# Attention and a maxout FFN in one kernel: batch 0 and its loads rearranged, and two pairs a turn from batch 2 on

## The chip, the cores and the metric

The kernel runs on one core of a Trainium2 chip. Five engines work in parallel, each with a queue of its own that it goes through in order: TensorE (PE: matmuls and transposes, results into PSUM), VectorE (DVE), ScalarE (ACT: exp, log), GpSimd (POOL) and SyncE (SP: issues DMAs). They wait for each other through semaphores. The metric is the device time of one execution in microseconds (us). Less is better.

## The reference

The inputs are q, k, v of 8 batches, 12 heads, 448 tokens and 64 dims. Attention has one more term in the denominator of the softmax, and its output is the input of an FFN with three up-projections, of which the largest counts:

```python
scores = q @ k.T / sqrt(64);  m = max(scores)
e = exp(scores - m)
attn = e / (sum(e) + exp(-m) + 1e-09)
x = (attn @ v), heads side by side        # 3584 x 768
h = maximum(maximum(x @ w1, x @ w2), x @ w3)
out = h @ w_out                           # all weights 768 x 768
```

Since exp(-m) is one more exponential of zero, the kernel works without the maximum: e / (sum(e) + 1) with e = exp(scores).

## The kernel before

**Pairs.** Work goes by pairs of heads: 6 pairs a batch, 48 in all, one to a turn of the main loop (`it`). The 448 keys of a head are 3 chunks of 128 and a last one of 64. Scores are made transposed (keys on the partitions). For a chunk of 128 keys two matmuls of 64 rows each run side by side on the two halves of the array, one per head: these are the half-array matmuls (64x448 in the profile; `scores`, L239). The last chunks of both heads go together as one matmul over the full array (`scores_last`, L255). `exp_scores` (L249) is one ScalarE exp of 896 columns per chunk, into `eT`; `exp_last` (L265) one of 448, into `eL`.

**Sums.** `av_main` (L273) multiplies with v and a block of ones beside it, so that one head's output and its denominator come out of the same six full matmuls. `av_last` (L285) adds the last chunk with two half-array matmuls. `reciprocals` takes 1/(sum+1) as exp(-ln(sum+1)) on ScalarE (L298, L299); `normalize` (L307, VectorE) writes the batch's `xT`. Batch 0 has a form of its own (`sums_main`, `sums_last`, `reciprocals_one`, `normalize_one`).

**FFN.** When a batch's six pairs are done, `batch_done` puts its groups on a list: 18 `up_group`s (six full matmuls each, L356, closed by VectorE with a copy, L370, or a maximum, L372) and 6 or 8 `out_group`s (six matmuls, L390, then VectorE, L415, and a DMA out). `group()` takes the next one off the list; the turns of the next batch call it 3 to 5 times, between the steps of attention, so that TensorE has work while ScalarE and VectorE finish. Batch 0 has no groups to fill in, and uses `keep_busy` (L349), matmuls on zeros.

**Queues.** The order on each engine is the order in which the program is written out (`manual_schedule`). q, k, v of a pair come by DMA from SP's queue (`load`, L92 and L93: two DMAs for each of q, k, v) into three raw buffers of three pairs each. Weights come from POOL's queue (`load_weight`, L147); they are converted to fp16 on the way. In the profile q1 is the DMA queue of SP and ScalarE, q0 that of POOL. VectorE casts q and k to fp16 (`cast_qk`: L183, L184, L189) and POOL scales v (`scale_v`, L157). Up to pair 11 TensorE transposes q and k (`transposes`, L221, L226; VectorE copies them out into `qkT`, L233); from pair 12 on a DMA does (L209).

**PSUM.** Three pools of two buffers: `s` (scores, also the last chunk's), `av` (sums), `u` (groups and transposes). A buffer comes free when its reader is done. A turn in the steady part of before is

```python
scores(p,0..1); group(); av_main(prev); av_last(prev)
scores(p,2); scores_last(p); reciprocals(prev); exps
group(); normalize; group(); normalize; further groups
```

The order in batch 0 (L470 to L508), the first turn of batch 1 (L509 to L530) and the initial loads (L97 to L114) is written out by hand.

Of the kernel before, what the change touches and what calls it, by code (L numbers as in the profile page):

```python
# [21 lines left out]
def kernel(  # L22
# [44 lines left out]
    out_pool = ctx.enter_context(tc.tile_pool(name="outp", bufs=3))  # L67
# [8 lines left out]
    NRAW = 3  # L76
    HB = NPAIR // 2
# [24 lines left out]
    load(1, 2, "v")  # L102
    load(3, 1, "qk")
    load(4, 2, "q")
    load(3, 1, "v")
    load(4, 2, "k")
# [6 lines left out]
    nc.vector.memset(raw[2][0][64:128, 0:2, NB, :], 0.0)  # L113
# [24 lines left out]
    eT = cpool.tile([128, 2, NB, 2, S], MMDT, name="eT")  # L138
# [22 lines left out]
    def casts(p):  # L161
        cast_qk(p)
        scale_v(p)

    def cast_qk(p):
        qt, kt, _ = raw[(p // HB) % NRAW]
        h0 = 2 * (p % HB)
        hs = slice(h0, h0 + 2)
        k6, q6 = k16[p % NK], q16[p % NK]
        if p == 0:  # L170

            nc.scalar.copy(out=k6[:, 0:NB], in_=kt[:, hs, 0:NB].rearrange("p h c d -> p c h d"))
            for eng, cs in ((nc.scalar.copy, slice(0, 2)), (nc.vector.tensor_copy, slice(2, NB + 1))):
                eng(out=q6[:, cs], in_=qt[:, hs, cs].rearrange("p h c d -> p c h d"))
        else:
            if p >= P_DMA and (p // NPAIR) % 2:

                nc.vector.tensor_copy(
                    out=q6[:, 1 : NB + 1], in_=qt[:, hs, 0:NB].rearrange("p h c d -> p c h d")
                )  # L180
                nc.vector.tensor_copy(out=q6[64:128, 0], in_=qt[0:64, hs, NB])
            else:
                nc.vector.tensor_copy(out=q6, in_=qt[:, hs].rearrange("p h c d -> p c h d"))  # L183
            nc.vector.tensor_copy(  # L184
                out=k6[:, 0:NB], in_=kt[:, hs, 0:NB].rearrange("p h c d -> p c h d")
            )
        for hh, half in enumerate(halves):
            last = nc.gpsimd if p == 0 else nc.vector
            last.tensor_copy(out=k6[half, NB, hh], in_=kt[0:64, h0 + hh, NB])  # L189
# [14 lines left out]
    def transposes(p):  # L204
        odd = (p // NPAIR) % 2
        qkT = att_pool.tile([2 * D, 1024], MMDT, tag="qkT", bufs=3)
        qkTs[p] = qkT, 0, S
        if p >= P_DMA:
            nc.sync.dma_start_transpose(  # L209
                out=qkT.rearrange("q (c p) -> q c p", p=128),  # L210
                in_=qk16[p % NK].rearrange("p c h d -> p (c h d)"),
            )
            qkTs[p] = qkT, 64 * odd, 512
            return
        trT = ps_u.tile([128, 1024], MMDT, tag="u", name="trT")


        order = (NB, 0, 1, 2) if odd else (0, 1, 2, NB)
        n0 = 0
        for c in order:  # L220
            nc.tensor.transpose(  # L221
                out=trT[:, n0 : n0 + 128], in_=q16[p % NK][:, c], identity=ident16
            )
            n0 += SL if c == NB else 128
        for c in range(NB + 1):
            nc.tensor.transpose(  # L226
                out=trT[:, S + c * 128 : S + c * 128 + 128], in_=k16[p % NK][:, c], identity=ident16
            )
        if p == 0:
            nc.vector.tensor_copy(out=qkT[:, 0 : S + 128], in_=trT[:, 0 : S + 128])  # L230
            nc.scalar.copy(out=qkT[:, S + 128 : S + 512], in_=trT[:, S + 128 : S + 512])
        else:
            nc.vector.tensor_copy(out=qkT[:, 0 : S + 512], in_=trT[:, 0 : S + 512])  # L233
# [14 lines left out]
    def exp_scores(p, c, stp):  # L248
        nc.scalar.activation(out=eT[:, p % 2, c], in_=stp[:, :, 0:S], func=AF.Exp, scale=scale)  # L249
# [13 lines left out]

    def exp_last(p, stl):
        nc.scalar.activation(out=eL[:, p % 2], in_=stl[:, 0, 0:S], func=AF.Exp, scale=scale)  # L265
# [3 lines left out]
    def av_main(p, hh, av=None):  # L269
        if av is None:  # L270
            av = ps_av.tile([128, 512], FP32, tag="av", name="av")
        for c in range(NB):
            nc.tensor.matmul(  # L273
                out=av[:, 0:S],
                lhsT=vst[:, p % VB, hh * NB + c, (1 - hh) * D : (3 - hh) * D],
                rhs=eT[:, p % 2, c, hh, :],
                start=(c == 0),
                stop=False,
            )
        return av  # L280
# [32 lines left out]
    def sums_main(p, ps, ones):  # L313
        for c in range(NB):
            for hh, half in enumerate(halves):
                nc.tensor.matmul(  # L316
                    out=ps[half, 0:S],
                    lhsT=vst[:, p % VB, hh * NB + c, (1 - ones) * D : (2 - ones) * D],
                    rhs=eT[:, p % 2, c, hh, :],
                    start=(c == 0),  # L320
                    stop=False,
                )
# [10 lines left out]
    def reciprocals_one(den):  # L333
        lnd = small.tile([128, S], FP32, tag="lnd")
        rb = small.tile([128, S], FP32, tag="rb")
        nc.scalar.activation(out=lnd, in_=den[:, 0:S], func=AF.Ln, bias=1.0)
        nc.scalar.activation(out=rb, in_=lnd, func=AF.Exp, scale=-1.0)
        return rb
# [108 lines left out]
    LEFT = 4  # L447
    keep_busy(13)
    casts(0)
    transposes(0)  # L450
    keep_busy(3)
    for it in range(NP + 1):
        p = it if it < NP else None
# [5 lines left out]
        first = {3: 1, 4: 2}.get(it)  # L459
        if first is not None:  # L460
            hs = slice(2 * first, 2 * first + 2)
            nc.vector.memset(raw[2][0][64:128, hs, NB - 1 : NB + 1, :], 0.0)
            if first == 1:
                load(NPAIR, 1, "v")
            load(NPAIR + first, 1)
        if it in (3, 4):
            load_weight(0, it - 3)
        if it in (5, 6, 8):
            load_weight((5, 6, 8).index(it) + 1)
        if it < NPAIR:  # L470

            casts(it + 1)
            for c in range(2):
                exp_scores(p, c, scores(p, c))
            if prev is None:
                keep_busy(3)
                exp_scores(p, 2, scores(p, 2))
                transposes(1)
                exp_last(p, scores_last(p))
            else:  # L480
                den, av = (ps_av.tile([128, 512], FP32, tag="av", name=n) for n in ("den", "av"))
                sums_main(prev, den, 1)
                stp = scores(p, 2)
                sums_main(prev, av, 0)
                stl = scores_last(p)
                sums_last(prev, den, 1)
                sums_last(prev, av, 0)
                exp_scores(p, 2, stp)
                exp_last(p, stl)
                rb = reciprocals_one(den)  # L490
                transposes(it + 1)
            if it < NPAIR - 1:
                keep_busy(3)
            else:

                ups = [up_open()]
                up_part(ups[0], 0, 0, 0, range(3))
                av5 = ps_s.tile([128, 2, 512], FP32, tag="s", name="av5")
                sums_main(p, av5[:, 1], 1)
                sums_main(p, av5[:, 0], 0)  # L500
                sums_last(p, av5[:, 1], 1)
                sums_last(p, av5[:, 0], 0)
                rb5 = reciprocals_one(av5[:, 1])
            if prev is not None:
                normalize_one(prev, av, rb)
            if it == NPAIR - 1:
                normalize_one(p, av5[:, 0], rb5)
                batch_done(0)  # L508
        elif it == NPAIR:  # L509
            exp_scores(p, 0, scores(p, 0))  # L510

            up_part(ups[0], 0, 0, 0, (3,))
            ups.append(up_open())
            up_part(ups[1], 0, 0, 1, range(4))
            ups.append(up_open(ps_av, "av"))
            up_part(ups[2], 0, 0, 2, range(4))
            for dc in (4, 5):
                for fc, ps in enumerate(ups):
                    up_part(ps, 0, 0, fc, (dc,))
                    if dc == 5:  # L520
                        up_close(ps, 0, 0, fc)
            del queue[0:3]
            exp_scores(p, 1, scores(p, 1))
            group()
            casts(it + 1)
# [5 lines left out]
        else:  # L531
            late = it + 1 < P_DMA
            if not late:

                if it + 2 < NP:
                    cast_qk(it + 2)
                    transposes(it + 2)
                if it + 1 < NP:
                    scale_v(it + 1)
            if p is not None:  # L540
                for c in range(2):
                    exp_scores(p, c, scores(p, c))
            group()
            if late:
                casts(it + 1)
            avs = [av_main(prev, hh) for hh in range(2)]
            av_last(prev, avs)
            if p is not None:
                stp = scores(p, 2)
                stl = scores_last(p)  # L550
            rb = reciprocals(prev, avs)
            if p is not None:
                exp_scores(p, 2, stp)
                exp_last(p, stl)
# [6 lines left out]
            if it % NPAIR == 0:  # L561
                batch_done(prev // NPAIR)
# [3 lines left out]
            for _ in range(n_groups - 3):  # L566
                group()

        for n in range(NPAIR + HB, 2 * NPAIR) if it == NPAIR else (it + 5,):
            if it >= NPAIR and n < NP:  # L570
                load(n, 1)
# [32 lines left out]
```

## Time and profile before

| | |
|---|---|
| median of 3 runs | 367.63 us (367.45 to 368.14) |
| the profiled execution | 367.07 us, span 365.3 us |
| TensorE busy | 357.4 us (98%) |
| VectorE busy | 243.4 us (67%) |
| ScalarE busy | 221.1 us (61%) |
| GpSimd busy | 53.6 us (15%) |
| up matmuls (L356) | 864, 175.3 us |
| out matmuls (L390) | 336, 59.3 us |
| sums with v (L273) | 252, 54.5 us |
| scores (L239) | 288, 44.1 us |
| keep-busy (L349) | 34, 10.1 us |
| DMA | 58.61 MB, mean 160 GB/s |

The span runs from the first to the last instruction. The shown duration of a matmul holds the time that it takes to pass through the array, and matmuls overlap: the time that one costs is read from the start of one to the start of the next. "Idle before" tells how long an engine stood still ahead of a group of instructions, and who released it.

### The profile page before, as it was taken

The numbers are of one execution on the slowest core, as the hardware profiler recorded it, in microseconds if no ns is written. First come the engines' busy times: TensorE is split into PE (matmuls) and PEld (weight loads), VectorE is DVE, ScalarE is ACT, GpSimd is POOL, SyncE is SP. The second block draws the span as 40 slices with busy tenths as digits, with TensorE's granted clock in tenths as the row PEclk, the third lists the DMA queues.
The fourth block names the chain that finished last, engine by engine and source line by source line (L and its number), as shares of the span: only waits on it lengthen the run. The fifth ranks groups of instructions, "written<-read, shape, count | busy, mean of one in ns | idle before, by whom it ended". The sixth has DMA issues, their size and how long they took to land.

```text
span 365.3 us, 6122 instructions
## 1 busy us (share of the span) xinstructions
PE 357.4 (98%) x2086; PEld 163.9 (45%) x2086; DVE 243.4 (67%) x521; ACT 221.1 (61%) x335; POOL 53.6 (15%) x159
## 2 busy tenths in 40 slices
PE   8999999999999999999999999999999999999995
PEld 3434444444444444444444444444444444445552
DVE  4474777876578677577657867757666776555553
ACT  4996476765666766666567666666566766651000
POOL 4263112211211211211121121121112112000000
PEclk9999999999999999999999999999999999999999
DMA  5999997668667888849764896758675673005006
GB/s 151 229 234 229 233 247 211 155 177 214 161 180 182 208 184 154 195 107 185 182 173 122 178 200 164 175 133 214 159 174 137 165 208 83 5 2 131 2 0 172
DMA packets 87951, 58.61 MB, mean 160 GB/s; under 512 B 43504, under 2 KB 84464, under 8 KB 87920
## 3 DMA queue, kind: packets, MB, share of 16 engines
q1 hardware_dynamic: 83632, 53.18, 59.7%
q0 software_dynamic: 3920, 4.72, 7.5%
q10 hardware_dynamic: 368, 0.33, 0.4%
q8 instruction: 16, 0.26, 0.3%
q14 instruction: 15, 0.12, 0.1%
HBM read 42.47 MB, written 11.01 MB: 146 GB/s over the span
## 4 chain that ended last, share of the span: by engine, by line
PE 91%; ACT 2%; DMA 2%; DVE 2%; issue 1%; SPq 0%; DVEq 0%
PE up L356 44%; PE op L390 15%; PE av L273 13%; PE stp L239 8%; PE stl L255 4%; PE av L285 3%; DMA kin<-in_k_dram 2%; PE busy L349 2%; ACT eT L249 1%; PE trT L221 1%; PE trT L226 1%; PE av L316 1%; DVE qkT L233 1%; DVE o_sb L415 0%; DVE qk L183 0%
## 5 line engine op out<-in xcount | busy, mean ns | idle before, releaser
L356 PE MATMUL up<-xT,w 128*128 128x448 f16 x864 | 175.3, 353 | 0.7 <-DVE xT L307 0.4
L249 ACT ACTIVATE eT<-stp 128x896 f16<-128x896 f32 x144 | 125.5, 910 | 53.3 <-PE stp L239 53.3
L356 PEld LDWEIGHTS <-w 128*128 128x128 f16 x864 | 81.7, 98 | 81.7 <-issue 12.5
L372 DVE TENSOR_TENSOR hT<-hT,up 128x448 f16<-128x448 f16 x96 | 59.6, 621 | 52.1 <-PE up L356 51.1
L157 POOL TENSOR_SCALAR vst<-vin 128x384 f16<-128x384 f32 x132 | 43.1, 338 | 255.2 <-issue 159.2
L298 ACT ACTIVATE lnd<-av 64x448 f32<-64x448 f32 x84 | 45.3, 539 | 49.0 <-PE av L285 48.0
L390 PE MATMUL op<-w,hT 128*128 128x384 f16 x336 | 59.3, 326 | 0.0
L273 PE MATMUL av<-eT,vst 128*128 128x448 f16 x252 | 54.5, 352 | 0.0
L307 DVE TENSOR_TENSOR xT<-av,rb 64x448 f16<-64x448 f32 x84 | 51.8, 617 | 1.4
L239 PE MATMUL stp<-qkT 64*128 64x448 f16 x288 | 44.1, 353 | 1.5 <-DVE qkT L233 0.7
L370 DVE CAST hT<-up 128x448 f16<-128x448 f32 x48 | 29.8, 624 | 22.9 <-PE up L356 22.2
L415 DVE TENSOR_SCALAR o_sb<-op 128x384 f32<-128x384 f32 (+1 forms) x56 | 30.8, 550 | 20.0 <-PE op L390 19.0
L390 PEld LDWEIGHTS <-hT 128*128 128x128 f16 x336 | 31.6, 98 | 24.7 <-issue 4.0
L273 PEld LDWEIGHTS <-vst 128*128 128x128 f16 x252 | 24.7, 98 | 22.4
L184 DVE CAST qk<-kin 128x384 f16<-128x384 f32 x47 | 25.7, 548 | 1.1 <-DMA kin<-in_k_dram 0.7
L265 ACT ACTIVATE eL<-stl 128x448 f16<-128x448 f32 x48 | 25.9, 539 | 0.0
L299 ACT ACTIVATE rb<-lnd 128x448 f32<-128x448 f32 x42 | 24.2, 576 | 1.3
L239 PEld LDWEIGHTS <-qkT 64*128 64x128 f16 x288 | 11.0, 94 | 23.2 <-issue 16.5
L419 ACT ACTIVATE o_sb<-op 128x192 f32<-128x192 f32 x1 | 0.3, 331 | 30.2 <-DVE o_sb L415 30.2
L189 DVE CAST qk<-kin 64x64 f16<-64x64 f32 x94 | 17.5, 187 | 1.3
L255 PE MATMUL stl<-qkT 128*128 128x448 f16 x48 | 17.4, 362 | 0.0
L285 PE MATMUL av<-eL,vst 64*128 64x448 f16 x84 | 15.2, 359 | 0.0
(50 smaller groups left out, 117.7 us busy)
## 6 DMA issues: line engine op xcount, KB each, us to landing
out_dram<-o_sb SPq DMA_DIRECT2D x54, 192.0 KB, 2.8
qin<-in_q_dram SPq DMA_DIRECT2D x46, 128.0 KB, 3.0
kin<-in_k_dram SPq DMA_DIRECT2D x45, 128.0 KB, 2.9
vin<-in_v_dram SPq DMA_DIRECT2D x44, 128.0 KB, 2.9
kin<-in_k_dram SPq DMA_DIRECT2D x46, 96.0 KB, 2.7
qin<-in_q_dram SPq DMA_DIRECT2D x45, 96.0 KB, 2.7
vin<-in_v_dram SPq DMA_DIRECT2D x44, 96.0 KB, 2.8
w<-in_moe_w_dram POOLq DMA_DIRECT2D x2, 1152.0 KB, 17.1
```

Source lines behind the costliest of these rows:

```text
L157: nc.gpsimd.tensor_scalar(out=out, in0=in_, scalar1=LAMBDA, scalar2=1.0, op0=ALU.mult, op1=ALU.mult)
L239: nc.tensor.matmul(out=stp[:, hh, 0:S], lhsT=qkT[hh * D : hh * D + D, k0 + c * 128 : k0 + c * 128 + 128], rhs=qkT[hh * D : hh * D + D, q0 ...
L249: nc.scalar.activation(out=eT[:, p % 2, c], in_=stp[:, :, 0:S], func=AF.Exp, scale=scale)
L255: nc.tensor.matmul(out=stl[:, 0, 0:S], lhsT=qkT[:, k0 + NB * 128 : k0 + NB * 128 + 128], rhs=qkT[:, q0 : q0 + S], start=True, stop=True,)
L273: nc.tensor.matmul(out=av[:, 0:S], lhsT=vst[:, p % VB, hh * NB + c, (1 - hh) * D : (3 - hh) * D], rhs=eT[:, p % 2, c, hh, :], start=(c == ...
L298: nc.scalar.activation(out=lnd[mine], in_=avs[hh][other, 0:S], func=AF.Ln, bias=1.0)
L307: nc.vector.tensor_tensor(out=xTs[b][mine, j, :], in0=avs[hh][mine, 0:S], in1=rb[mine], op=ALU.mult)
L356: nc.tensor.matmul(out=ps[:, 0:S], lhsT=w_sb[i][:, dc, ts(fc, 128)], rhs=xTs[b][:, dc, :], start=(dc == 0), stop=(dc == NDC - 1),)
L370: nc.vector.tensor_copy(out=h, in_=ps[:, 0:S])
L372: nc.vector.tensor_tensor(out=h, in0=h, in1=ps[:, 0:S], op=ALU.max)
L390: nc.tensor.matmul(out=ps[:, 0:NW], lhsT=hTs[sb][:, fc, ts(t, 128)], rhs=wout_sb[:, fc, ts(nh, NW)], start=(fc == 0), stop=(fc == NFC - 1),)
L415: nc.vector.tensor_scalar(out=o_sb[:, cs], in0=src, scalar1=1.0 / LAMBDA, scalar2=None, op0=ALU.mult)
```

## The change

**Loads and buffers.** The raw buffers become four of two pairs each (`NRAW`, `HB`), the output tiles five instead of three, `eT` three instead of two. The initial loads take v of pairs 1 and 2, and k of pairs 4 and 5, one by one (four DMAs more on SP), and k of 4 and 5 stands before v of 3. Pair 7's q and k, then v of 6 and 7, then pair 8's q and k are issued in turns 4, 5 and 6, each behind a small VectorE memset of a part of the tile that the load then writes. v of 8 and 9 and q, k of 9 follow in turn 7; from turn 8 on every load is of two pairs.

**Weights.** The first half of w1 is issued on POOL in turn 3 behind `scale_v(3)` and a VectorE memset of one of its columns, the second half at the start of turn 4, w2, w3 and w_out at the start of turns 5, 6 and 8. `scale_v(p)` moves from turn p-1 into turn p, up to pair 11.

**Batch 0.** In turn p the next pair's transposes and its first scores are written out before the sums of the previous pair with v; the normalise moves into the next turn; `keep_busy` stays in turn 0 alone. Pair 5's sums, the first three up groups of batch 0 and pair 6's transposes (in a buffer of the `s` pool) follow each other in turn 5. Pair 4's transposes are copied out in two parts.

**From pair 12 on** a turn takes two pairs. The half-array matmuls stand in three stretches: `av_last(p-1)` with scores 0 and 1 of p; score 2 of p with score 0 of p+1; `av_last(p)` with scores 1 and 2 of p+1. The last chunks of both pairs share one PSUM buffer and one exp (`scores_last2`, `exp_last2`). A turn calls `group()` 8 to 10 times.

The diff, cut:

```diff
-    NRAW = 3
-    HB = NPAIR // 2
+    NRAW = 4
+    HB = 2
...
     load(2, 1, "qk")
-    load(1, 2, "v")
+    load(1, 1, "v")
     load(3, 1, "qk")
+    load(2, 1, "v")
     load(4, 2, "q")
+    load(4, 1, "k")
+    load(5, 1, "k")
     load(3, 1, "v")
-    load(4, 2, "k")
     load(4, 2, "v")
...
+    def scores_last2(p):
+        stl = ps_s.tile([128, 2, 512], FP32, tag="s", name="stl")
+        for n in range(2):
+            qkT, q0, k0 = qkTs[p + n]
+            nc.tensor.matmul(
+                out=stl[:, n, 0:S],
+                lhsT=qkT[:, k0 + NB * 128 : k0 + NB * 128 + 128],
+                rhs=qkT[:, q0 : q0 + S],
...
+    def exp_last2(stl):
+        nc.scalar.activation(out=eL, in_=stl[:, :, 0:S], func=AF.Exp, scale=scale)
...
-        first = {3: 1, 4: 2}.get(it)
-        if first is not None:
-            hs = slice(2 * first, 2 * first + 2)
-            nc.vector.memset(raw[2][0][64:128, hs, NB - 1 : NB + 1, :], 0.0)
-            if first == 1:
-                load(NPAIR, 1, "v")
-            load(NPAIR + first, 1)
-        if it in (3, 4):
-            load_weight(0, it - 3)
+        if it in (4, 5, 6):
+            t = (raw[NRAW - 1][0], raw[NRAW - 1][2], raw[0][0])[it - 4]
+            hs = slice(0, 2) if it == 6 else slice(2, 4)
+            nc.vector.memset(t[64:128, hs, NB - 1 : NB + 1, :], 0.0)
+            p_new, n_new, names = ((NPAIR + 1, 1, "qk"), (NPAIR, 2, "v"), (NPAIR + 2, 1, "qk"))[it - 4]
+            load(p_new, n_new, names)
+        if it == 4:
+            load_weight(0, 1)
         if it in (5, 6, 8):
             load_weight((5, 6, 8).index(it) + 1)
...
+                last = it == NPAIR - 1
+                late = it == 3
+                if last:
+                    normalize_one(*waiting)
+                else:
+                    cast_qk(it + 1)
+                scale_v(it)
+                if late:
+                    nc.vector.memset(w_sb[0][:, 0, 0:1], 0.0)
+                    load_weight(0, 0)
+                elif waiting is not None and not last:
+                    normalize_one(*waiting)
+                exp_scores(p, 1, scores(p, 1))
                 den, av = (ps_av.tile([128, 512], FP32, tag="av", name=n) for n in ("den", "av"))
                 sums_main(prev, den, 1)
                 stp = scores(p, 2)
-                sums_main(prev, av, 0)
+                if not late and not last:
+                    transposes(it + 1)
                 stl = scores_last(p)
                 sums_last(prev, den, 1)
-                sums_last(prev, av, 0)
                 exp_scores(p, 2, stp)
                 exp_last(p, stl)
-                rb = reciprocals_one(den)
-                transposes(it + 1)
-            if it < NPAIR - 1:
-                keep_busy(3)
+                lnd = log_one(den)
+                if late:
+                    transposes(it + 1)
+                    normalize_one(*waiting)
+                if not last:
+                    exp_scores(it + 1, 0, scores(it + 1, 0))
+                    waiting = prev, av, exp_one(lnd)
+                sums_main(prev, av, 0)
+                sums_last(prev, av, 0)
...
-        for n in range(NPAIR + HB, 2 * NPAIR) if it == NPAIR else (it + 5,):
-            if it >= NPAIR and n < NP:
-                load(n, 1)
+        if it == NPAIR + 1:
+            load(it + 1, 2, "v")
+            load(it + 2, 1, "qk")
+        elif it in (8, 9):
+            for p_new in ((10,), (12, 14))[it - 8]:
+                load(p_new, 2)
+    avs = [av_main(P_DMA - 1, hh) for hh in range(2)]
+    for p in range(P_DMA, NP, 2):
...
+        av_last(p - 1, avs)
+        stps = [scores(p, c) for c in range(2)]
+        rb = reciprocals(p - 1, avs)
+        for c in range(2):
+            exp_scores(p, c, stps[c])
+        group()
+        normalize(p - 1, 0, avs, rb)
+        group()
+        normalize(p - 1, 1, avs, rb)
+        if p % NPAIR == 0:
+            batch_done(p // NPAIR - 1)
+        group()
+        exp_last2(scores_last2(p))
+        if more:
+            cast_q(p + 2)
+        for _ in range(n_groups - 7):
+            group()
+        if more:
+            cast_k(p + 2)
+            transposes(p + 2)
+        scale_v(p + 1)
+        stps = [scores(p, 2), scores(p + 1, 0)]
+        exp_scores(p, 2, stps[0])
+        exp_scores(p + 1, 0, stps[1])
+        group()
+        if more:
+            cast_qk(p + 3)
+            transposes(p + 3)
+            scale_v(p + 2)
+        if p + 6 < NP:
+            load(p + 6, 2)
+        avs = [av_main(p, hh) for hh in range(2)]
+        av_last(p, avs)
+        stps = [scores(p + 1, c) for c in (1, 2)]
+        rb = reciprocals(p, avs)
+        for c in (1, 2):
+            exp_scores(p + 1, c, stps[c - 1])
+        group()
+        for hh in range(2):
+            normalize(p, hh, avs, rb)
+        group()
+        group()
+        avs = [av_main(p + 1, hh) for hh in range(2)]
```

## The prediction

> **What bounds the kernel now.** I read the page's first part and its chain, then TensorE's rows in order of time, first in the steady part, then in batch 0, then the DMA queues in short windows.
>
> ```profile
> PE 357.4 (98%) x2086; PEld 163.9 (45%) x2086; DVE 243.4 (67%) x521; ACT 221.1 (61%) x335; POOL 53.6 (15%) x159
> PE 91%; ACT 2%; DMA 2%; DVE 2%; issue 1%; SPq 0%; DVEq 0%
> ```
>
> TensorE is the bound, and from 42 us on it waits for nobody (its wait list holds 2.6 us, all of it before 42). So a gain must take time out of TensorE's own row, and any new wait there is lost in full. One pair in the steady part, TensorE in order of time (start, us):
>
> ```profile
> 207.22 0.55 PE L239 MATMUL stp<-qkT 64*128 64x448 f16 x4
> 207.71 1.31 PE L356 MATMUL up<-xT,w 128*128 128x448 f16 x6
> 208.85 1.30 PE L273 MATMUL av<-eT,vst 128*128 128x448 f16 x6
> 210.08 0.36 PE L285 MATMUL av<-eL,vst 64*128 64x448 f16 x2
> 210.28 0.35 PE L239 MATMUL stp<-qkT 64*128 64x448 f16 x2
> 210.57 0.36 PE L255 MATMUL stl<-qkT 128*128 128x448 f16 x1
> 210.77 3.57 PE L356 MATMUL up<-xT,w 128*128 128x448 f16 x18
> ```
>
> Read the starts, not the second column, which holds the pipeline's tail. Six full matmuls take 208.85-207.71 = 1.14 (0.19 each). Six take 1.23 when a half-array one (64x448) follows, two half ones 0.20, but 0.29 when a full one follows (210.28 to 210.57), four 0.49 instead of 0.38. So each step between full and half array costs 0.09 to 0.10 us. One pair has two half-array stretches, so four steps, 0.38 us.
>
> Batch 0, one pair, ScalarE:
>
> ```profile
> 15.09 2.53 ACT L249 ACTIVATE eT<-stp 128x896 f16<-128x896 f32 x3 [0.28 <-PE stp L239]
> 17.50 0.56 ACT L265 ACTIVATE eL<-stl 128x448 f16<-128x448 f32 x1
> 17.92 0.57 ACT L336 ACTIVATE lnd<-den 128x448 f32<-128x448 f32 x1
> 18.53 0.58 ACT L337 ACTIVATE rb<-lnd 128x448 f32<-128x448 f32 x1
> 19.39 0.92 ACT L249 ACTIVATE eT<-stp 128x896 f16<-128x896 f32 x1 [0.28 <-PE stp L239]
> ```
>
> 4.30 us a pair, of which ScalarE waits 0.28 for scores. TensorE fills up with three keep-busy matmuls and a wait of 0.18 for qkT.
>
> DMA, window 33 to 37 us (packets, MB, share), then the two loads of pair 9's k with their time to landing (issued at 36.11 and 37.52), then weight 1 (issued at 25.96), then VectorE's cast of pair 9:
>
> ```profile
> q0 software_dynamic: 388, 0.60, 81.6%
> q1 hardware_dynamic: 389, 0.32, 31.7%
> ```
>
> ```profile
> kin<-in_k_dram SPq DMA_DIRECT2D x1, 128.0 KB, 11.4
> kin<-in_k_dram SPq DMA_DIRECT2D x1, 96.0 KB, 11.2
> ```
>
> ```profile
> w<-in_moe_w_dram POOLq DMA_DIRECT2D x1, 1152.0 KB, 14.9
> ```
>
> ```profile
> 51.08 0.54 DVE L184 CAST qk<-kin 128x384 f16<-128x384 f32 x1
> 51.54 0.40 DVE L189 CAST qk<-kin 64x64 f16<-64x64 f32 x2
> ```
>
> While weights (q0) are in flight they take 0.15 MB/us and the q, k, v loads (q1) get 0.08, packet for packet. Pair 9's k lands at 48.7, 2.4 us before its cast, and its transposes start on TensorE at 51.91. This margin decides the case.
>
> **Two pairs a turn, from pair 12.** 36 pairs have 4 stretches per two pairs, then 3 per turn: (A) second-half sums of p-1 with scores 0, 1 of p; (B) score 2 of p with score 0 of p+1; (C) sums of p with scores 1, 2 of p+1. 18 turns lose one stretch, two steps, 0.19 us: **-3.4 us**. The matmuls are the same in number.
>
> New waits inside a turn, from the steps of the same rows (groups of six up 1.14, of six op 0.98; exp of 896 0.83; two Ln 1.10, exp 0.58). After stretch A starts, ScalarE does Ln, exp, two score exps, free at 3.7. TensorE: stretch 0.69, three groups, the last-block scores at 4.1 (3.6 if op). Their merged exp ends at 5.6 (5.2); stretch B's second score needs that buffer at 5.9 (5.3). It holds by 0.1 to 0.3, five turns being of the tight kind: 0 to 0.5 us in all, I take 0. Before av_main of p+1 two normalises must clear the sums: VectorE is done at 3.8 after C, TensorE wants the second at 4.7. The merged exp (one of 0.83 for two of 0.43) is off the path, ScalarE is at 61%. The DMA transposes (3.0 to landing) are issued 7 us into a turn of 14, and used at its end, 6 us of cover; past loads of two pairs SP issues 6 instead of 12 DMAs a turn. If that cover went, the first scores of each turn would wait. I take 0.
>
> Third eT slot, five output buffers, split casts: no extra time, hidden under TensorE's groups.
>
> **Batch 0.** With the next pair's transposes and score 0 moved ahead of the sums, ScalarE's 0.28 wait per pair goes: 4.02 a pair. Keep-busy drops from 34 matmuls to 22. The third exp of pair 5 would end at 29.2 rather than 30.5. Then TensorE does pair 5's sums, 18 up matmuls, pair 6's transposes and pair 7's turn starts at about 40.9 (now 42.0): **-1.1**; -0.3 if pair 4's k is late (VectorE waits 0.40 for k at 21.30 now), -1.35 if all of ScalarE's gain comes through. I take the middle of the two rows that limit it, TensorE's own work after pair 5. The twelve keep-busy matmuls that go (12 x 0.19 = 2.3) are not counted again: where they stood, TensorE would wait for ScalarE anyway. Next late is the load side.
>
> **Weights and loads.** First weight half: POOL now issues it behind scale_v(3). v of pair 3 stands four DMAs later in SP's list (0.65 us each), so it lands at about 21.6, is scaled in 1.05, and the weight goes at 22.6 (now 19.67). Data first move 2.2 us later in the rows (no q0 packets before 21.8), so 24.9. The new memset of a weight column, which POOL's issue waits for, is done on VectorE near 21, ahead of that, so it holds up nothing (scale_v(4) is what stands behind it). The other half and weights follow 1 to 5 us later, w_out behind scale_v(7) at about 40: q0 never runs dry, which it does now between 46 and 49.4 (0.35 MB where 0.51 would be the rate; q1 got 0.57). So q0 runs from 24.9 for 4.72/0.15 = 31.5 us, to 56.4. Weight 0's first half lands at 29, wanted 31.5; weight 1 at 40.7, wanted 41.4: no wait, but 0.7 of cover (now 1.6).
>
> q1 in that time gets 0.08. Up to 24.9 it has landed what SP issued by 22.1: pairs 0 to 5, q and half k of 6, 4384 KB = 4.49 MB. Pair 9's k now stands behind pairs 0 to 7 whole, q, k of 8, v of 8 **and 9** in one load, q of 9: 6720 KB = 6.88 MB. (6.88-4.49)/0.079 = 30.3: it lands at 55.2 instead of 48.7. Window rows of 22 to 26 and 28 to 32 give 0.07 and 0.09: 51 to 57 (from 56.4 on the loads have the engines alone). The new gates on SP's queue (a memset before pair 7's q, v of 6 and 7, pair 8's q) hold back all loads behind them; the last one opens at 37.1, after pair 0's last up-closes on VectorE. It costs nothing by itself, since q1 is backlogged to about 40. From landing to transposes 0.1 + 0.83 (51.08 to 51.91): T(9) at **56.1**. Wanted 44.5 (pair 8) + 6.35 = 50.8. So TensorE stalls some 5 us, with nothing queued to fill in: it runs in order, and the groups behind the transposes wait too. Against now (51.91) pair 9 is 4.2 late, and the 1.1 of batch 0 is swallowed. Pair 10's k lands by 60, wanted 62.6: no second stall.
>
> **Sum.** -3.4 + 4.2 = **+0.8**. The profiled execution has 367.07 (span 365.3): 367.9. It stands 0.56 under the median of the runs, 367.63, so 368.4 for the median. 0.2% is 0.74 us, about what a measurement of this kernel can tell.
>
> **Rivals** (all on the median).
> (B) Loads come in time. Each 0.1 MB more on q1 by then is worth 1.3 us, and q0 ran dry twice in the trace of before; such a gap of 2 us at full rate brings k back to 52. Faster from a landing before 53.7; with no stall at all -3.4-1.1 = 363.1. For it: the margin is small bytes at a slow rate. Against: the weights are now queued well ahead of each other.
> (C) As forecast, and TensorE drops to half speed after the stall. The trace shows it starting slow: 13 keep-busy matmuls from 1.16 to 6.06, 0.38 each where later ones take 0.19, so 2.45 us lost in 4.9. The same after the stall gives up to 370.9. Against: no idle gap in before is longer than 1.2, so nothing shows that 5 us are enough.
> The Trainium skill, "TensorE: Matmul & The Clock Gate", Part 1, says that an idle window of about 3.4 us, free-running, puts the array back to half clock, and a like time of work lifts it; by it a stall of 5 us would hold a whole window about half the time. No run here shows it yet.
> (D) Stretch B waits in every turn because the merged exp is late: 0.5 us late would be 18 x 0.4 = 7 us on top, 375. The steps above speak against it.
> (E) The stretches merge but the steps cost the same, because the drain falls on the next group: gain 0, 371.8. The 0.20 between two half-array rows speaks against it.
>
> **Chances.** Forecast (landing 53.7 to 57) 0.45, of which 0.13 falls within 0.2%; B 0.38; C 0.12; D and E 0.05. Faster 0.38, same 0.13, slower 0.49. The forecast alone spans 366.9 to 370.3; the range reaches into B to 363.6 and through C to 371.2, which leaves out about 0.05 below and 0.09 above.
>
> **What would show it.** Right: TensorE's first transposes of pair 9 wait several us for VectorE's cast, which waits for kin; from pair 12 on three 64x448 stretches per 14 us turn and no idle; the windows of 33 to 50 hold q0 at 0.15 MB/us. Wrong: no kin wait near 51 to 56 (B), matmuls of 0.38 after it (C), stp waiting for ACT eL in each turn (D).

## The result

| | before | after |
|---|---|---|
| median | 367.70 us (367.45 to 368.14) | 372.75 us (372.38 to 372.90) |
| the profiled execution | 367.07 us, span 365.3 | 372.75 us, span 371.0 |
| TensorE busy | 357.4 us (98%) | 355.6 us (96%) |

The change is slower: ratio 1.0135, 95% interval 1.0117 to 1.0152. The predicted 368.4 had the direction right and was 4.35 us short; the range ended at 371.2.

The page of the kernel after: the engines' busy time, the shares of the chain that ended last, and the granted TensorE clock in 40 slices (9 is full speed).

```profile
PE 355.6 (96%) x2074; PEld 166.6 (45%) x2074; DVE 244.4 (66%) x525; ACT 219.5 (59%) x317; POOL 54.2 (15%) x159
PE 83%; DMA 7%; DVE 4%; SPq 4%; issue 1%; ACT 0%; DVEq 0%
PEclk9999996999999999999999999999999999999999
```

TensorE's share of the chain fell from 91% to 83%, and DMA and SP's queue now carry 11%. One slice of the clock, the seventh (55.7 to 64.9 us), is below full. TensorE's waits in the kernel after (total us, times, longest), without two that before has at the same places:

```profile
PE trT L241 <- DVE qk L193: 3.3, 3, 2.5
PE trT L236 <- DVE qk L188: 1.9, 1, 1.9
PE stp L257 <- DVE qkT L251: 1.8, 4, 0.6
PE up L394 <- DMA w<-in_moe_w_dram: 0.9, 1, 0.9
PE av L308 <- DVE xT L342: 0.6, 1, 0.6
```

The transposes (`trT`) wait for VectorE's casts, and these wait for q and k. All but the last line lie before 64 us. TensorE of the kernel after in order of time (the brackets: idle before, releaser; rows between are left out at the dots). The first row is the start of pair 7's turn:

```profile
42.11 0.55 PE L257 MATMUL stp<-qkT 64*128 64x448 f16 x4
43.56 1.31 PE L394 MATMUL up<-xT,w 128*128 128x448 f16 x6 [0.90 <-DMA w<-in_moe_w_dram]
...
47.46 0.54 PE L241 MATMUL trT<-ident,qk 128*128 128x128 f16 x4 [0.45 <-DVE qk L193]
...
50.21 0.55 PE L257 MATMUL stp<-qkT 64*128 64x448 f16 x4
...
55.84 0.40 PE L236 MATMUL trT<-ident,qk 128*128 128x128 f16 x4 [1.92 <-DVE qk L188]
58.78 0.61 PE L241 MATMUL trT<-ident,qk 128*128 128x128 f16 x4 [2.54 <-DVE qk L193]
59.18 4.68 PE L394 MATMUL up<-xT,w 128*128 128x448 f16 x12
63.79 0.55 PE L257 MATMUL stp<-qkT 64*128 64x448 f16 x4
```

The same starts in the kernel before, those of pairs 7, 8 and 9:

```profile
42.01 0.55 PE L239 MATMUL stp<-qkT 64*128 64x448 f16 x4
...
48.37 0.55 PE L239 MATMUL stp<-qkT 64*128 64x448 f16 x4
...
52.36 2.43 PE L356 MATMUL up<-xT,w 128*128 128x448 f16 x12
54.73 0.55 PE L239 MATMUL stp<-qkT 64*128 64x448 f16 x4
```

Compare the three starts. Pair 7's turn: 42.11 against 42.01. Pair 8's: 50.21 against 48.37. Pair 9's: 63.79 against 54.73, 9.06 us late, and the whole span is 5.7 us longer. So all of the loss is made by 63.79, and from there to the end the kernel after is 3.4 us faster. Of the 9.06, 1.84 was there at pair 8's turn already, and 1.92 and 2.54 are the waits for q and k of pair 9. Then 12 up matmuls take 4.61 from start to start, where the same 12 took 52.36 to 54.73 = 2.37 before: half speed, 2.24 more.

The steady part of the kernel after, one turn of two pairs, in part:

```profile
209.21 0.36 PE L320 MATMUL av<-eL,vst 64*128 64x448 f16 x2
209.41 0.54 PE L257 MATMUL stp<-qkT 64*128 64x448 f16 x4
209.88 3.10 PE L428 MATMUL op<-w,hT 128*128 128x384 f16 x18
...
214.27 0.55 PE L257 MATMUL stp<-qkT 64*128 64x448 f16 x4
...
217.13 0.36 PE L320 MATMUL av<-eL,vst 64*128 64x448 f16 x2
```

Three half-array stretches (209.21, 214.27, 217.13) where two turns of before have four, and no bracket anywhere.

Now the DMA queues (packets, MB, share of the engines; q1 is SP's, with q, k and v, q0 POOL's, with the weights; the two loads that ScalarE issues at the start are on a queue of their own, q10). The kernel after, 40 to 42 us:

```profile
q0 software_dynamic: 283, 0.42, 115.8%
```

There is no line for q1: not one packet of q, k or v moved in these two microseconds. The kernel after, 42 to 56 us:

```profile
q0 software_dynamic: 1396, 2.11, 82.3%
q1 hardware_dynamic: 1389, 1.14, 31.7%
```

Packet for packet again, 0.15 and 0.08 MB/us. In the same window of before q0 moved 1.94 MB in 1285 packets and q1 1.43 in 1792, since q0 ran dry in between. Pair 9's k in the kernel after, issued at 42.78 and 43.89 (last number: us to landing):

```profile
kin<-in_k_dram SPq DMA_DIRECT2D x1, 128.0 KB, 13.9
kin<-in_k_dram SPq DMA_DIRECT2D x1, 96.0 KB, 14.2
```

It landed at 56.7 and 58.1. Before, it had landed at 48.7; the prediction said 55.2.

### The profile page after: what moved, and what is told of

Its sections match the earlier page's. It is cut to its first block, busy times and chain, and to the rows that moved or that the text cites. A ratio compares the mean times of both kernels' runs of the same rounds, so it can differ in the third digit from the quotient of the medians.

```text
span 371.0 us, 5887 instructions
## 1 busy us (share of the span) xinstructions
PE 355.6 (96%) x2074; PEld 166.6 (45%) x2074; DVE 244.4 (66%) x525; ACT 219.5 (59%) x317; POOL 54.2 (15%) x159
## 4 chain that ended last, share of the span: by engine, by line
PE 83%; DMA 7%; DVE 4%; SPq 4%; issue 1%; ACT 0%; DVEq 0%
PE up L394 43%; PE op L428 14%; PE av L308 12%; PE stp L257 7%; DMA kin<-in_k_dram 5%; PE av L320 3%; SPq L92 2%; SPq L93 2%; PE stl L287 2%; DMA qin<-in_q_dram 2%; DVE xT L342 1%; DVE o_sb L453 1%; DVE qk L193 1%; PE av L351 1%; PE trT L241 0%
## 5 line engine op out<-in xcount | busy, mean ns | idle before, releaser
L394 PE MATMUL up<-xT,w 128*128 128x448 f16 x864 | 177.4, 356 | 1.5 <-DMA w<-in_moe_w_dram 0.9
L408 DVE CAST hT<-up 128x448 f16<-128x448 f32 x48 | 29.1, 621 | 24.9 <-PE up L394 24.3
L257 PE MATMUL stp<-qkT 64*128 64x448 f16 x288 | 41.4, 352 | 2.0 <-DVE qkT L251 1.8
L297 ACT ACTIVATE eL<-stl 128x896 f16<-128x896 f32 x18 | 16.5, 917 | 14.2 <-PE stl L287 14.2
L257 PEld LDWEIGHTS <-qkT 64*128 64x128 f16 x288 | 12.6, 94 | 20.2 <-issue 12.1
L201 DVE CAST qk<-kin 64x64 f16<-64x64 f32 x94 | 20.7, 220 | 1.3
L188 DVE CAST qk<-qin 128x512 f16<-128x512 f32 x29 | 12.6, 436 | 7.0 <-DMA qin<-in_q_dram 6.2
```

The lines of the kernel that those rows point to most:

```text
L257: nc.tensor.matmul(out=stp[:, hh, 0:S], lhsT=qkT[hh * D : hh * D + D, k0 + c * 128 : k0 + c * 128 + 128], rhs=qkT[hh * D : hh * D + D, q0 ...
L394: nc.tensor.matmul(out=ps[:, 0:S], lhsT=w_sb[i][:, dc, ts(fc, 128)], rhs=xTs[b][:, dc, :], start=(dc == 0), stop=(dc == NDC - 1),)
L408: nc.vector.tensor_copy(out=h, in_=ps[:, 0:S])
```

## The experiments

The medians stand beside the kernel before on the same chip, 367.5 to 367.8 us, and every ratio is to that. Line numbers are those of each kernel. "Gate" in the expectations is the small memset that holds up SP's queue.

### What the turns of two pairs are worth

**e2_rest_only**: the kernel after with one pair a turn from pair 12 on.

```diff
-    for it in range(P_DMA):
-        p = it
+    for it in range(NP + 1):
+        p = it if it < NP else None
```

> The changed kernel with its loads, weights, raw buffers and batch 0, but one pair a turn from pair 12 on, as before. Theory (loads and weights cost 9.1 us at the start of pair 9's successor, 63.79 instead of 54.73, and the turns give back 3.4): 372.75 + 3.4 = 376.2. Rival (the turns take part in the loss): 373 or less.

Measured 376.60 us, ratio 1.0242 (1.0214 to 1.0270), as the theory had it. Against 372.75 the turns are worth 3.9 us inside the kernel after, beside the 3.4 of the traces.

**e1_turns_only**: the kernel before with the turns of two pairs and the third `eT` slot. The raw buffers of three pairs stay, so a turn issues its loads one pair at a time. The three output tiles stay as well.

```diff
+        for n in (p + 5, p + 6):
+            if n < NP:
+                load(n, 1)
```

> The kernel before with nothing of the change but the turns of two pairs from pair 12 on (and the third eT slot that they need); loads, raw buffers, weights and batch 0 as before. Theory (the turns save 3.4 us, and the loss lies in the loads and weights of batch 1): 367.7 - 3.4 = 364.3, TensorE without a wait after 84 us, 55 half-array stretches from pair 12 on instead of 73. Rival (the turns bring waits of their own and are a part of the loss): 366 or more.

Measured 386.50, ratio 1.0521 (1.0496 to 1.0546): far off the expectation. TensorE's largest wait in e1_turns_only, and one case of it:

```profile
PE up L391 <- DVE o_sb L450: 12.9, 3, 4.5
...
128.47 2.40 PE L391 MATMUL up<-xT,w 128*128 128x448 f16 x6 [4.53 <-DVE o_sb L450]
```

VectorE's copy into an output tile at 127.86 had itself waited 5.34 us for the DMA out of that tile. SP had issued 12 loads (115.92 to 124.2) ahead of that DMA. The tiles ran out because SP was late. The array also went to half speed at each of the three waits (see below).

**e5_turns_bufs5**: the same with five output tiles.

```diff
-    out_pool = ctx.enter_context(tc.tile_pool(name="outp", bufs=3))
+    out_pool = ctx.enter_context(tc.tile_pool(name="outp", bufs=5))
```

> The first experiment's kernel (before, with turns of two pairs and nothing else) and five output tiles instead of three. Theory (its 18.9 us came from the output tiles: two pairs' loads, 12 DMAs of 0.65 us, stand ahead of the output DMAs on SP's queue, VectorE waits for a free tile, and TensorE stood idle for 12.9 us in three turns and went to half speed after each): with five tiles the waits on o_sb go and the turns' own gain shows, 367.6 - 3.4 = 364.2. Rival (the turns cost by themselves, the tiles are a side effect): above 370.

Measured 375.14, ratio 1.0179 (1.0151 to 1.0206). 11.4 us came back, but the turns still did not pay. TensorE's largest wait in e5_turns_bufs5, and one case with the row behind it:

```profile
PE stp L257 <- DMA qkT<-qk: 7.4, 5, 2.2
...
308.47 0.55 PE L257 MATMUL stp<-qkT 64*128 64x448 f16 x4 [1.76 <-DMA qkT<-qk]
308.95 5.26 PE L391 MATMUL up<-xT,w 128*128 128x448 f16 x18
```

Now the DMA transposes, also on SP, came late. In a turn of 14 us SP issues 12 loads (0.65 each), two transposes (1.3 each) and 6 to 8 outputs (0.6): 14 to 15 us. SP had become the bound of these turns. (The 18 matmuls take 3.58 elsewhere in this run; on the 5.26 see below.)

**e6_after_bufs3**: the kernel after with three output tiles, the edit of e5 the other way round (two executions).

> The changed kernel with three output tiles instead of five. Theory: there 6 load DMAs of two pairs, 4 us of SP's queue, stand ahead of the output DMAs instead of 12, so some of the waits of the first experiment come: slower than 372.75 by 2 to 12 us, with VectorE's o_sb waiting for output DMAs. Rival (the six longer DMAs leave room enough): 372.75.

Measured 380.70, ratio 1.0354 (1.0336 to 1.0372): 8 us more than the kernel after, again with waits of an up group for an output tile (3 times, 6.7 us).

**e9_turns_whole**: the kernel before in batch 0, weights and order, with the turns, five output tiles, raw buffers of two pairs and loads of two pairs.

```diff
-    NRAW = 3
-    HB = NPAIR // 2
+    NRAW = 4
+    HB = 2
...
-    load(1, 2, "v")
+    load(1, 1, "v")
+    load(2, 1, "v")
...
+        if p + 6 < NP:
+            load(p + 6, 2)
```

> Before's batch 0, weights and order of loads, with the whole of what the turns turned out to need: turns of two pairs from pair 12 on, five output tiles, raw buffers of two pairs and loads of two pairs from pair 16 on (6 DMAs a turn on SP instead of 12). Theory (the turns are worth 18 stretches of 0.19 us, once neither output tiles nor DMA transposes are held up on SP's queue): 367.6 - 3.4 = 364.2, no wait of TensorE after 80 us. Rival (a wait stays, on qkT or o_sb): 366 or more.

Measured 368.18, ratio 1.0010 (0.9998 to 1.0022): no change, 4 us above the theory. The waits of e5 are gone after 92 us. But v of pairs 1 and 2 one by one is two more DMAs ahead of k of 4 and 5, and batch 0 waits for k of pair 4. TensorE in e9_turns_whole:

```profile
23.75 0.54 PE L245 MATMUL trT<-ident,qk 128*128 128x128 f16 x4 [1.57 <-DVE qk L200]
```

**e11_loads_only**: e9 without the turns.

> The same without the turns: before, with five output tiles, raw buffers of two pairs and loads of two pairs from pair 16 on, one pair a turn. Theory (the buffers and loads only make room, the stretches bring the gain): 367.6, as before. Rival (fewer DMAs on SP are a gain of their own): 366 or less.

Measured 369.40, ratio 1.0051 (1.0038 to 1.0064): 1.8 above the theory. The same wait is 1.88 us here, and the pair behind it takes 5.63 us instead of 4.30, at half speed. From the start of pair 7's turn to the end, e9 takes 321.7, and e11 and before 323.3. So in that kernel the turns gave 1.6 with 1.4 us of new waits for the first transposes inside them; 3.0 without these.

### Where the loss comes from

**e7_wout_late**: the kernel after with the last weight issued two turns later.

```diff
-        if it in (5, 6, 8):
-            load_weight((5, 6, 8).index(it) + 1)
+        if it in (5, 6, 10):
+            load_weight((5, 6, 10).index(it) + 1)
```

> The changed kernel with the last weight's load written out two turns later, so that POOL issues it behind v of pair 9, near 53 instead of 40. Theory (pair 9's k is late because the loads share the DMA engines with weights from 25 to 59): the loads have the engines alone from 51, k of pair 9 lands near 54 instead of 58, the idle stretch is some 1 us instead of 5 and the array stays at full speed: 372.75 - 3.9 - 2.2 = 366.6. Rival (order and gate of the loads on SP decide, the last weight does not): 371 or more.

Measured 366.86, ratio 0.9976 (0.9965 to 0.9987): 5.9 us faster than the kernel after, by one number. Pair 9's k in e7_wout_late:

```profile
kin<-in_k_dram SPq DMA_DIRECT2D x1, 128.0 KB, 10.8
kin<-in_k_dram SPq DMA_DIRECT2D x1, 96.0 KB, 10.1
```

It landed at 53.7, TensorE waited 0.57 us for it, and all up matmuls ran at full speed. So it was the last weight that took the engines from pair 9's loads. What it leaves is a wait of 1.58 us for weight 1.

**e10_no_gate**: the kernel after without the memset that held pair 8's q, and with it all loads behind, until 38.15.

```diff
-            nc.vector.memset(t[64:128, hs, NB - 1 : NB + 1, :], 0.0)
+            if it < 6:
+                nc.vector.memset(t[64:128, hs, NB - 1 : NB + 1, :], 0.0)
```

> The changed kernel without the memset ahead of pair 8's q, nothing else. The prediction took that gate to cost nothing; the trace shows the load queue empty from 40 to 42 because of it. Theory (0.25 MB more by then at 0.08 MB/us): k of pair 9 lands 3 us sooner, near 55, the idle stretch shrinks below 2 us and the array stays at full speed; weight 1 lands about 1.2 later for it: 372.75 - 3 - 2.2 + 0.5 = 368. Rival (the load queue is behind anyway, as predicted): 372 to 373.

Measured 368.97, ratio 1.0028 (1.0017 to 1.0040): the memset cost 3.8 us. The queue no longer empties. e10_no_gate, 40 to 42 us, where the kernel after had no line for q1, and TensorE behind the start of pair 7's turn:

```profile
q1 hardware_dynamic: 201, 0.16, 32.0%
...
45.44 1.67 PE L394 MATMUL up<-xT,w 128*128 128x448 f16 x6 [2.16 <-DMA w<-in_moe_w_dram]
46.91 2.44 PE L308 MATMUL av<-eT,vst 128*128 128x448 f16 x6
```

Pair 9's k is cast at 55.66, about where the prediction had it land, and no half speed follows it. Weight 1 is later for it: a wait of 2.16, and behind this wait a window at half speed (six `av` matmuls take 2.38 from start to start instead of 1.23). The 3.8 and the 5.9 of e7 don't add up: each edit by itself frees pair 9's k, and the whole loss was 5.05.

**e4_k9_first**: as e10, and q and k of pair 9 ahead of v of 8 and 9.

```diff
-            load(it + 1, 2, "v")
             load(it + 2, 1, "qk")
+            load(it + 1, 2, "v")
```

> The changed kernel with two edits to its loads: q and k of pair 9 ahead of v of 8 and 9, and no memset gate before pair 8's q. Theory (pair 9's k is late by its place in the queue and by the gate): k lands near 50 instead of 58, the stall at pair 9 (4.5 us), its half-speed stretch (2.25) and pair 8's 0.45 go; weight 1 lands some 1.4 later because the loads no longer pause at 40, so its wait grows from 0.9 to about 2.3: 372.75 - 7.2 + 1.4 = 367.0. Rival (the bytes beside the weights are the limit, whatever their order): the wait moves to pair 10's k, about 2 us there, 369.

Measured 370.26, ratio 1.0053 (1.0026 to 1.0080), above both numbers that were expected. The wait moved on, as the rival said. TensorE in e4_k9_first, at weight 1 and at pair 10's transposes:

```profile
44.96 1.31 PE L394 MATMUL up<-xT,w 128*128 128x448 f16 x6 [2.15 <-DMA w<-in_moe_w_dram]
...
63.69 0.54 PE L241 MATMUL trT<-ident,qk 128*128 128x128 f16 x4 [1.92 <-DVE qk L193]
64.07 4.08 PE L394 MATMUL up<-xT,w 128*128 128x448 f16 x12
```

Another order hands the shortage to another pair; only fewer bytes before the deadline remove it.

### Half speed after a wait

**e3_hold_clock**: the kernel after with 24 matmuls on zeros ahead of pair 9's transposes. They make TensorE busy while it waits, and bring no load sooner.

```diff
+            if it == 8:
+                keep_busy(24)
```

> The changed kernel with 24 keep-busy matmuls (4.5 us) on TensorE ahead of pair 9's transposes, where it stands idle from 53.8 to 58.8 but for four transposes. Theory (idle time puts the array to half speed, the 12 up matmuls after it take 4.68 us instead of 2.43): the wait for pair 9's k stays, the half-speed stretch goes, 372.75 - 2.25 = 370.5. Rival (the array is slowed by something else at that time, such as the DMA traffic): 372.7, with the up matmuls behind the transposes still at 0.39 each.

Measured 370.70, ratio 1.0099 (1.0066 to 1.0131): 2.05 us less than the kernel after. TensorE in e3_hold_clock:

```profile
54.15 4.70 PE L387 MATMUL busy<-idle 128*128 128x448 f16 x24
...
59.31 2.43 PE L394 MATMUL up<-xT,w 128*128 128x448 f16 x12
```

The same 12 up matmuls, at nearly the same time, take 2.43 instead of 4.68. The lost speed is due to the idle time, not to the DMA traffic.

When does the clock fall? In e1_turns_only it fell three times. Stretches of that run, TensorE's busy time first, the granted clock behind the engines:

```profile
127.75:128.00 0.25, 0.00 (x0) 0.00 (x0) 0.14 (x1) 0.00 (x0) 0.00 (x0) 0.99 0.70 197
128.00:131.25 3.25, 2.78 (x8) 1.13 (x8) 2.83 (x8) 0.00 (x0) 0.00 (x0) 0.50 0.62 199
131.25:131.50 0.25, 0.25 (x2) 0.09 (x1) 0.25 (x2) 0.00 (x0) 0.00 (x0) 0.68 1.04 221
216.50:216.75 0.25, 0.00 (x0) 0.00 (x0) 0.00 (x0) 0.00 (x0) 0.00 (x0) 0.99 1.17 356
305.25:305.50 0.25, 0.00 (x0) 0.00 (x0) 0.00 (x0) 0.00 (x0) 0.00 (x0) 0.98 0.96 246
```

A mean of 0.99 in a quarter of a microsecond puts the fall at its very end: 127.99, 216.74 and 305.49, 88.75 us apart both times. The mean of 0.68 puts the return at 131.41, 3.42 us after the fall; the third lasted 6.82, twice that, and 88.75 is 26 times 3.413. So the clock is set on a fixed grid of 3.41 us. The Trainium skill, "TensorE: Matmul & The Clock Gate", Part 1, gives a free-running window of 3413 ns, and these edges agree. It has the clock fall after at least one idle window; here windows that were partly busy were enough. In e4_k9_first, on the grid that its fall at 64.69 fixes:

```profile
40.80:44.21 3.41, 1.78 (x10) 0.60 (x9) 1.37 (x3) 1.54 (x2) 0.45 (x1) 1.00 1.15 233
44.21:47.62 3.41, 2.66 (x16) 1.21 (x16) 1.31 (x3) 0.18 (x1) 0.00 (x0) 1.00 1.15 233
61.28:64.69 3.41, 1.40 (x12) 0.81 (x13) 1.29 (x5) 2.08 (x4) 0.00 (x0) 1.00 1.11 236
64.69:68.10 3.41, 3.41 (x12) 1.13 (x12) 1.39 (x3) 0.00 (x0) 0.95 (x3) 0.50 1.13 232
```

The wait of 2.15 us that ended at 44.96 lies across an edge, 1.40 in one window and 0.75 in the next; TensorE is busy 1.78 and 2.66, and the clock stays. The wait of 1.92, shorter, lies in one window, together with the last 0.10 of another wait; TensorE is busy 1.40, and the next window runs at 0.50, although TensorE was at work at the edge. The same reading for other windows, each on the grid of a fall in its own run:

| window | TensorE busy, of 3.41 us | clock in the next window |
|---|---|---|
| after, 53.48 | 0.83 | 0.50 |
| e10, 42.84 | 1.25 | 0.50 |
| e6, 130.39 | 1.31 | 0.50 |
| after, 56.89 | 1.53 | 0.50 |
| e6, 51.88 | 1.62 | 1.00 |
| e11, 22.36 | 1.63 | 0.50 |
| e5, 306.00 | 1.65 | 0.50 |
| e6, 304.46 | 2.01 | 1.00 |
| e6, 215.72 | 2.04 | 1.00 |
| e5, 220.67 | 2.06 | 1.00 |

With the two of e4 these are twelve windows. Eleven fit one line between 1.65 and 1.78, about half a window; the 1.62 of e6 doesn't, so TensorE's busy time in the trace, where the ends of matmuls are modelled, gives the line only roughly. In e10 a wait of 2.16 lies whole in one window, and half speed follows; in e4 the wait of 2.15 lies across an edge, and none does. The kernel after had two such windows in a row (53.48 and 56.89), so two at half speed, of which the second, 60.31 to 63.72, was all work.

### Batch 0, and a faster order

**e8_loads_mended**: the kernel after with e4's and e7's edits, the first weight half ahead of v of pair 3, and q and k of pair 4 ahead of 5's.

```diff
-    load(4, 2, "q")
-    load(4, 1, "k")
-    load(5, 1, "k")
+    load(4, 1, "qk")
+    load(5, 1, "qk")
```

> The changed kernel with its loads mended: q and k of pair 4 ahead of pair 5's, the first weight half on POOL ahead of v of pair 3 (still behind VectorE's cast of pair 4), no gate before pair 8's q, q and k of pair 9 ahead of v of 8 and 9, the last weight two turns later. Theory (the turns and batch 0's chain are sound, loads and weights alone lost the time): no wait of TensorE over 0.6 us after 42, pair 7 starts near 41 instead of 42.1, and the time is 367.6 - 3.4 - 1.1 = 363.1. Rival (each mend moves the lack of DMA time to another transfer): weight 1 or pair 9 or 10 waits, 365 to 368.

Measured 366.41, ratio 0.9969 (0.9953 to 0.9985), the rival's number. Pair 4's first scores start at 21.46, where the kernel after has 22.32, so q and k of pair 4 were late there. But three waits are new or longer in e8_loads_mended:

```profile
PE up L393 <- DMA w<-in_moe_w_dram: 1.4, 1, 1.4
PE op L427 <- DMA w<-in_moe_w_out_dram: 1.3, 1, 1.3
PE av L350 <- POOL vst L158: 1.3, 1, 1.3
```

Each load put first made another late: weight 1, w_out, v.

**e12_weights_sooner**: the kernel after with moves on POOL's queue alone: the first weight half ahead of `scale_v(3)`, w2 and w3 a turn sooner, w_out two turns later.

```diff
-        if it in (5, 6, 8):
-            load_weight((5, 6, 8).index(it) + 1)
+        if it in (4, 5, 10):
+            load_weight((4, 5, 10).index(it) + 1)
...
-                scale_v(it)
                 if late:
                     nc.vector.memset(w_sb[0][:, 0, 0:1], 0.0)
                     load_weight(0, 0)
-                elif waiting is not None and not last:
+                scale_v(it)
+                if not late and waiting is not None and not last:
                     normalize_one(*waiting)
```

> The changed kernel with the weights alone moved on POOL's queue: the first half ahead of v of pair 3 (still behind VectorE's cast of pair 4), the second weight and the third one turn sooner, the last one two turns later. Loads and gates as changed. Theory (with the last weight out of the way, what is left is the wait for weight 1, 1.6 us; starting the weights 1.4 us sooner takes it away): 366.9 - 1.6 = 365.3. Rival (the loads pay for it: v of 4 and 5 or k of 8 comes later and TensorE waits there): 366 to 367.

Measured 365.92, ratio 0.9963 (0.9950 to 0.9975): the lowest median here (e8's 366.41 is too near to tell apart), 1.6 us below before and 6.8 below after. The wait for weight 1 is gone, and the rival's came, for pair 8's k. TensorE in e12_weights_sooner:

```profile
47.44 0.54 PE L241 MATMUL trT<-ident,qk 128*128 128x128 f16 x4 [1.59 <-DVE qk L193]
```

Pair 9's turn starts at 56.54, 1.8 us later than before, and -3.4 + 1.8 = -1.6 is its gain.

## Why the prediction was wrong

The direction was right for the reason given, a stall at pair 9. Two steps of the sum failed, and they are nearly all of the miss. The prediction put pair 9's first transposes at 56.1, so its turn at 56.1 + 2.82 = 58.9 (51.91 to 54.73 before). It came at 63.79, 4.9 us later, and the profiled execution at 372.75 instead of 367.9, also 4.9.

- **"It costs nothing by itself, since q1 is backlogged to about 40": wrong, some 2.45 us.** The backlog itself ended nearly as said. By 24.9 us, 4.48 MB had moved (q1 4.25, q10 0.23; said 4.49), and 1.16 MB came from there to 39, 0.08 MB/us. That makes 5.64 MB, all that was issued ahead of the memset (pairs 0 to 7 and 128 KB of pair 8's q). What the step put at nothing is the time from an issue to its first packet. The memset let SP go on at 38.15 (said 37.1), and the next packets of q1 moved at 42.0, 3.9 us after the issue. By the prediction's own times 2.9 of these were covered; but the memset was 1 us later and the backlog ended 1 us sooner, and some 3 us passed without a packet, 3 x 0.08 = 0.24 MB. k landed 2.9 us behind the forecast, and its transposes started 2.45 late: 58.78, where the forecast has 56.1 for q's and 0.23 more for k's, 56.33. e10 shows the step by itself: without the memset 3.8 us less, and k where the forecast had it.
- **The rate beside weights, 0.08 MB/us: right on average only.** From 30 to 36 us q0 moved 906 packets, 0.73 MB (0.8 KB each, mostly the halves of the first weight), and q1 845 packets, 0.70 MB. The row of before at 33 to 37 us has 388 of 0.60 MB (1.5 KB each) against 389 of 0.32. The Trainium skill, "DMA: Bandwidth & Descriptors", Queues, rings and completion order, says that an engine takes queues in turn by packets; 1396 against 1389 agrees. With equal numbers of packets, the size of a packet sets the share of the bytes.
- **Rival C was given 0.12, and happened on top: 2.4 us.** The sum had no term for it. 12 up matmuls at half speed cost 2.24, the transposes ahead of them 0.18. "No idle gap in before is longer than 1.2" was read as evidence against; it only meant that before could not show it. Two waits of 1.92 and 2.54 were enough, and e5 shows that a single one of 1.76 can be.

Other steps:

- **The turns, -3.4: right.** From 63.79 on the trace gives -3.4; e2 gives 3.9 by medians. No wait inside the turns, as D said against itself.
- **The shortage at pair 9: right in place and cause**, by e7 (5.9 us for the last weight's place).
- **"Weight 1 at 40.7, wanted 41.4: no wait": wrong.** It landed at 43.5, since q0 too got only 0.73/6 = 0.12 MB/us while the halves moved, and TensorE waited 0.90. In the kernel after this costs nothing more, because the stall at pair 9 ends by k's landing; in e7 and e10 it is a loss of its own (1.58, 2.16).
- **Batch 0, -1.1: wrong, +0.1.** The chain ran as said (3.94 us from the scores of one pair to those of the next, said 4.02). But VectorE waited for q and k of pair 4, until 20.0 and 20.6, and this held the transposes; e8 gives 0.86 back there. The lower end, -0.3, was named for this reason. The stall at pair 9 would have swallowed the gain anyway, as the prediction said.
- **"Third eT slot, five output buffers, split casts: no extra time": right, but half the story.** They were costed as an addition. e6 shows that the turns need them (8 us), e5 that they need the loads of two pairs as well (SP's 14 to 15 us of issues a turn). The halved issues stood in the prediction only as cover for the transposes.

## What to carry to other kernels

When transfers share the DMA engines, make a list of bytes by deadline, with the rate of each stretch from its own packets, and send what isn't wanted yet later: w_out two turns later was worth 5.9 us, while another order among the loads only moved the wait. Only a backlog hides a gate on a queue: work out when the backlog ends, and let the gate open earlier than that by the time from an issue to its first packet (here some 4 us). Count the issues on a DMA-issuing queue per turn as on any engine, and price a wait of TensorE of 1.7 us or more at up to another 1.7 us for half speed in the next window (waits of 1.57 to 1.59 in e7, e9 and e12 cost nothing more).

## What was not expected of the hardware

- The clock falls after a window that is more than about half idle (busy 0.83 to 1.65 of 3.41 us fell, 1.78 to 2.06 did not, and neither did one of 1.62). Since the grid runs on its own, a wait of 2.2 us may cost nothing more (e4) or a window at half speed (e10). It goes with this that the spread of e4 follows the granted clock: the executions at 0.998 and 0.999 took 368.1 to 368.9 us, those at 0.990 to 0.995 took 370.3 to 371.4.
- From SP's issue at 38.15 to the first packets on the empty queue some 4 us passed, with q0 at 0.21 MB/us meanwhile.

Left open: a kernel that has the whole 3.4 us of the turns without a wait before pair 9 (an estimate: 367.7 - 3.4, some 364 us) was not reached. Every order tried for the loads and weights before 60 us left at least 1.3 us of waits somewhere.
